# Linear attention with a soft MoE: late guards for the first three units, phases of the first batch carried on by TensorE, a new order of issue

## The chip, the cores and the metric

The kernel runs on one core of a Trainium2 chip. The time is device microseconds of one execution; three runs of the kernel before took 287.93 to 288.15 us, with a median of 288.11 us. "PE" is TensorE with its weight loads shown apart as "PEld", "DVE" is VectorE, "ACT" is ScalarE, "POOL" is GpSimd and "SP" is SyncE, whose queue issues nearly all DMAs here.

## What is computed

The reference is a gated linear attention with complex gates, followed by a soft mixture of experts. Cut to what matters:

```python
mag = sqrt(a_re**2 + a_im**2);  scale = minimum(mag, 0.999) / (mag + 1e-6)
a = scale * (a_re + 1j * a_im)                   # a gate for each token and channel
for t in range(768):                             # S is 48 x 48 for each batch and head
    S = a[t][:, None] * S + outer(k[t], v[t])
    y[t] = q[t] @ S.real
# 4 batches, 8 heads, 48 channels; y becomes x of 3072 tokens x 384
logits = x @ phi                                 # 32 slots = 8 experts x 4
slot_input = softmax(logits, 0).T @ x
slot_out = relu(slot_input @ w1[e]) @ w2[e]      # w1 384 x 1024, w2 1024 x 384
out = softmax(logits, 1) @ slot_out
```

## The kernel before, in words

**Blocks and units.** The recurrence is turned into blocks of 128 tokens. There are 24 blocks `g` (6 for each batch, `NBLK`), and three blocks make a unit `u` (`UB = 3`, 8 units). In a block the gates are used in polar form: the logarithm of the magnitude and the phase are summed over the tokens by a triangular matrix on TensorE, and q and k are multiplied by the exponentials and by the cosine and sine of the sums. Then scores, masked scores times v, and a state that is handed from block to block are ordinary matmuls.

**Gates of a unit (`gates`, L635 to L670).** The real and imaginary parts `ar` and `ai` lie in the tile `aat` (two buffers). The steps are a guard; `Ln` of `ar` in place (ACT, L647); `Exp` of its negative into the tile `gt` (ACT, L649); `ai` times that (DVE, L651); its square with a running maximum (DVE, L653); `Ln` of one plus the square (ACT, L655); their sum (DVE, L657); `Exp` (ACT, L659); and the cap (DVE, L661). `gt` has a single buffer. The guard (L642 on DVE for the first two groups, L645 on ACT for the others) reads `ar` before the logarithm overwrites it and leaves a minimum, or a sum that is zero when all is well. The first unit is gated in two groups, block 0 alone and blocks 1 and 2 together; every other unit is one group, so there are nine (`g0` to `g8`). At the end `flags` reduces the guards to one number; a branch to a slow version of the kernel hangs on it.

**Phases (`arctan`, `phase`).** After an arctangent (ACT, L677) a block's phases are summed by `up = tri_u x ph` (PE, L688), rounded (`n`, L692 or L694), and the fraction `f` is taken (DVE, L697). Sine and cosine are two ACT instructions and one DVE instruction (L702, L705, L707). A block that isn't the first of its batch needs the last block's fraction: DVE adds the last row of `f` of block g-1 to the first row of `ph` (L685, one partition), and then comes the matmul.

**Exponentials, products, attention.** `expo` is the matmul `lp` (L719, later L722) and two `Exp` (L726, L728); its last row goes by a small DMA to `rows` and comes back as `rt` (`decay`, L731, L735). `mults` makes the 128x1536 tile `hat` (DVE, L742, L747). `xpose` transposes it on PE (L759) and evicts it into `hT` (ACT, L765, DVE for block 0, L763). `score` is L770 with the masked eviction `scT` (DVE, L774), `attend` is L795 and L797 with the eviction L800, `delta` the update of the state (L808, L813, L815), `xform` a transpose of the result (L820).

**Mixture.** `logits`, `slots` and `shares` run once for a unit, then `hidden` (`H`, L241), `experts` (`X`, L271) and `combine` (`A`, L300), and twelve stores (`S`, L976).

**What sets the order.** The string `ORDER` is the order of issue, written out. Each name is one step of a generator: `p1` is the next step of `phase` for block 1, `g2` of the gates' group 2, `e`, `m`, `x`, `c`, `a`, `D` are the functions above, `T` and `L` load ScalarE's table for trigonometry or for logarithm and exponential, `la`, `lq`, `lv` load a unit's gates, q and k, and v, `w` loads 1 MB of expert weights, `d` is `decay`, and `wu` is a matmul on zeros without use ("warm-up"). `_InOrder` pins every instruction behind the one before it on its engine. So each engine and each queue runs strictly in this order and waits for the others by semaphores. PSUM tiles come from two rings: `tr` with four buffers, and `lu` with two, which `up`, `lp`, the logits and the small transposes share. Weights go through the pool `wx` with eight buffers, then through buffers that `aat`, `qkt` and other pools leave free.

Of the kernel before, what the change touches and what calls it, by code (L numbers as in the profile page):

```python
# [11 lines left out]
F32 = mybir.dt.float32  # L12
# [3 lines left out]
ALU = mybir.AluOpType  # L16
# [24 lines left out]
SPLIT, GUARD_V, ROUND_V, COPY_V = 4, 2, 4, 1  # L41
# [54 lines left out]
class _Moe:  # L96
# [216 lines left out]
    wu6 wu4 wu1 L0 wu12 wu18 i0 g0 g0 g0 g0 g0 wu17 i3 g0 g0 wu5 g0 i4 g1 g1 g1 rp1 i1 g0 e0 e0 e0 wu3 wu9 T0 t0 g1 g1 t1 e0 i2  # L313
    m0 p0 p0 p0 p0 p0 p0 L1 p1 g1 p1 m0 g1 i7 g1 wu16 i6 wu2 p1 p1 g1 p2 rp0 D0 x2 x2 p2 p2 x3 x3 p2 la0 g2 g2 g2 g2 g2 e1 e1 e1
    wu0 x1 x1 e2 e2 e2 x0 g2 T1 p1 wu14 lv0 wu10 p2 t2 D0 x0 c0 g2 c0 la1 p1 p1 p2 p2 wu15 m1 a0 p3 wu7 L2 m1 c1 c1 p3 p3 g2 g2
    x4 x4 a0 a0 x5 x5 wu13 m2 p3 e1 e2 g3 e3 e3 wu8 g3 c2 e3 g3 e5 e5 d0 m2 x10 x10 x9 e5 i8 p4 p4 x11 x11 c2 x6 x9 D0 D1 p4 x6
    g3 g3 x7 g3 x7 D1 p4 D1 p5 e4 lq0 g3 x8 x8 wu11 m3 p5 e4 e4 p5 p5 D2 c3 g3 D2 c5 c3 T2 e3 rp1 t3 p3 p3 p3 a1 a1 p6 D1 la2 p5
    p5 g3 e6 c5 p4 p5 p4 c4 m3 x12 lq1 x13 e4 D2 c4 a1 p6 m4 D3 D3 a2 p6 a2 m5 p7 p4 m4 x12 x13 D2 c6 x14 g4 c6 L3 a2 D3 l0 l0
    l0 g4 w0 e5 e6 g4 g4 e6 x14 x16 x16 x19 x19 D4 e8 x18 e8 e8 x15 x15 p7 x18 p7 g4 g4 x17 a3 x17 m5 s0 p7 p8 e7 f0 f0 g4 q0 q0
    e6 e7 e7 d1 D3 g4 f2 f2 c7 c7 c8 c8 p8 la3 q0 q0 s0 T3 p8 x20 lv1 m6 t4 lq2 p8 p7 a3 p7 p7 a3 x21 D4 p6 p6 c9 p8 x23 p9 e7  # L320
    s0 c9 p9 p6 x20 q0 a4 a4 x21 tr0 g4 m6 q0 x23 x22 x22 q0 rp0 p8 p9 c10 w1 c10 p8 D4 x27 x27 a4 g5 L4 x26 x26 s0 x25 x25 e8
    g5 c11 x24 x24 p9 D5 D5 g5 e9 m8 e9 e9 c11 e10 e10 d2 D4 a5 a5 m7 f1 f1 e10 lv2 m7 x31 x31 x28 x28 c13 m8 p10 p10 g5 g5 p10
    a5 c12 x30 p10 x29 c12 g5 e11 x29 l1 a6 x30 c13 p11 l1 a6 g5 e11 e11 m11 c14 lq3 D5 q1 q1 x34 a6 g5 c14 x34 p11 p11 m9 q1 q1
    c15 c15 T4 t5 f3 x33 p9 p10 la4 f3 D6 D6 x35 x35 p11 s0 p9 p9 D6 D6 p12 l1 p11 p11 x32 p10 s0 m9 x32 f4 f4 g5 p11 p10 a7 a7
    p12 D7 D7 q1 x33 L5 p12 m10 e9 e10 e11 c16 c16 c17 s1 a7 p13 g5 x36 x36 D7 D7 x37 x37 x38 D8 g6 c17 x38 a8 a8 g6 m10 g5 c18
    c18 q1 g6 q1 g6 g6 x42 x42 x43 x41 x41 x39 x39 e12 x43 e12 e12 D8 D8 p13 p13 p13 f5 f5 m11 x40 g6 g6 c19 c19 e14 lv3 e14 e14
    p14 d3 c21 e13 x40 D8 m12 D9 c20 e13 e13 e12 x44 s1 e13 s1 a8 a9 a9 g6 T5 c20 x44 c21 a9 p14 p14 t6 x46 x46 g6 p12 p12 D9 D9
    D9 g6 x45 x45 p14 p12 p14 p15 f7 p13 p13 p13 l2 m13 f7 l2 a10 a10 a10 m12 w2 f6 f6 c22 c22 p15 q2 p15 x47 x47 p14 p14 la5 g7
    p15 g6 x50 x50 p15 p15 p15 e14 D10 D10 lq4 d4 x51 p16 D10 c23 c23 L6 w3 x48 x51 q2 x49 m13 e15 e15 e15 x48 e15 g7 m14 m14
    a11 a11 c25 c25 p16 D11 p16 p16 D11 g7 g7 x49 p17 e16 e16 e16 x55 x57 x55 a11 e17 g7 e17 c24 e17 D11 c24 x57 l2 x54 x54 x56  # L330
    D11 p17 p17 l3 p17 g7 g7 q2 q2 l3 x52 x52 s1 x53 a12 a12 x53 x56 s1 lv4 c27 c27 la6 s1 s2 c26 c26 m15 g7 x58 x59 f8 c28 a12
    e16 a13 a13 T6 p17 p17 t7 x59 p18 p16 D12 g7 p17 p16 x58 c29 p18 a13 w4 m15 q2 D12 p16 f8 m17 x61 w5 p18 s2 c29 g8 c28 p19
# [8 lines left out]
    f17 f17 x84 x84 c41 D17 x85 c41 x86 x85 a20 x86 L9 a20 a20 m22 x88 x87 s4 m23 D18 x89 x88 D17 D18 c42 x89 x87 c43 e23 d7 D18
    q5 q5 l6 c42 w10 c43 l6 m23 a21 a21 a21 q6 D19 x92 q5 x92 q5 q6 q6 q6 x90 x90 x94 x91 q5 x91 x93 x94 D19 D18 D19 q6 c44 c44
    x95 s5 s5 c45 l6 c45 q6 D19 s5 q6 x93 c46 a22 a22 c46 x95 c47 c47 a22 a23 a23 a23 s6 s5 s5 s5 l7 l7 l7 f19 f19 q7 q7 s6 s6
    f20 f20 q7 f23 f23 q7 s7 me0 me0 s6 s6 f22 i5 s6 f21 s7 s7 f22 s7 er1 me0 f21 s7 me0 me0 me0 me0 er0 s7 ze0 q7 q7 w13 w12
# [200 lines left out]
def _polar(ctx, tc, cst, phi_sb, rp, bad, aa, qk, vv, phi, w1, w2, consts, out):  # L545
# [30 lines left out]
    amiss = cp.tile([P, len(GROUPS) - GUARD_V], F32, name="amiss")  # L576
    amin = cp.tile([P, GUARD_V], F32, name="amin")
# [57 lines left out]
    def gates(x):  # L635
# [5 lines left out]
        if x < GUARD_V:  # L641
            DVE.tensor_scalar(out=t, in0=ar, scalar1=AR_MIN, scalar2=None, op0=ALU.max, op1=ALU.min, accum_out=amin[:, x : x + 1])  # L642
        else:
            y = x - GUARD_V
            ACT.activation(out=t, in_=ar, func=AF.Relu, scale=-1.0, bias=kb[:, 3:4], accum_out=amiss[:, y : y + 1])  # L645
        yield "g1"
# [24 lines left out]

    cs, fr = {}, {}
# [6 lines left out]
    def phase(u, j):  # L679
        g = UB * u + j  # L680
        par = g % 2
        ph = aat[u][:, j, 1]
        r = slice(FIRST[par], FIRST[par] + 1)
        if g % NBLK:
            DVE.scalar_tensor_tensor(out=ph[r], in0=fr[g - 1][r], scalar=-2.0 * math.pi, in1=ph[r], op0=ALU.mult, op1=ALU.add)  # L685
            yield "p1"
        up = ps2.tile([P, HD], F32, name="up", tag="lu")
        PE.matmul(out=up, lhsT=tri_u[par], rhs=ph, start=True, stop=True)  # L688
        yield "p2"
        n = eo.tile([P, HD], F32, name="n")  # L690
        if g < ROUND_V:
            DVE.tensor_scalar(out=n, in0=up, scalar1=MAGIC, scalar2=None, op0=ALU.add)  # L692
# [9 lines left out]
        ACT.activation(out=t[:, :, 1, :], in_=f.rearrange("p (h d) -> p h d", d=D), func=AF.Sin, scale=-TWO_PI)  # L702
# [139 lines left out]
    for g in range(NG):  # L842
# [135 lines left out]
    def flags():  # L978

        good = tl.tile([P, 5], F32, name="good")  # L980
        t1 = tl.tile([P, 6], F32, name="good1")
        DVE.tensor_reduce(out=t1[:, 0:1], in_=tmax, axis=AX.X, op=ALU.max)
        DVE.tensor_reduce(out=t1[:, 1:2], in_=amiss, axis=AX.X, op=ALU.max)
        DVE.tensor_reduce(out=t1[:, 5:6], in_=amin, axis=AX.X, op=ALU.min)
# [126 lines left out]
```

## Time and profile before

| what | value |
|---|---|
| median of three runs | 288.11 us (287.93 to 288.15) |
| profiled execution | 288.15 us, of which the span is 286.3 us |
| PE busy, share of the span | 270.5 us, 94% |
| PEld busy | 216.3 us, 76% |
| DVE busy | 231.7 us, 81% |
| ACT busy | 219.3 us, 77% |
| granted clock, mean | 0.983 |
| DMA | 54.84 MB, mean 192 GB/s |
| matmul records on zeros (L923) | 38, 22.5 us busy |

The busy shares are means over stages: a start of some 40 us in which one unit's chain of steps runs with gaps, a long middle, and an end with the experts and the stores. The chain of waits tells which work ended last; the busy time of each engine in stretches tells which engine is full where. A matmul in float32 appears as two records, a transpose as one. Matmuls overlap in the records, so what one costs in a dense stream is the distance between starts, as the chain shows it, and not the duration of one record.

### The profile page before, as it was taken

How to read it: one execution, taken by the hardware profiler on the slowest of the kernel's cores; microseconds unless marked ns; L12 is line 12 of the kernel's file. 1: busy time of each engine (PE TensorE's matmuls, PEld its weight loads, DVE VectorE, ACT ScalarE, POOL GpSimd, SP SyncE). 2: the span in 40 equal slices, each digit the busy share in tenths (PEclk: the TensorE clock that was granted, in tenths of full speed). 3: DMA queues.
4: the chain of work that ended last, by engine and by line, in shares of the span. 5: the costliest groups of instructions: out<-in, count | busy, mean ns of one | idle time of the engine just before them, and what ended most of it. 6: DMA issues, size and time to landing. Idle time of an engine off the chain costs nothing.

```text
span 286.3 us, 6873 instructions
## 1 busy us (share of the span) xinstructions
PE 270.5 (94%) x2825; PEld 216.3 (76%) x2825; DVE 231.7 (81%) x422; ACT 219.3 (77%) x396; POOL 4.8 (2%) x11
## 2 busy tenths in 40 slices
PE   8869899999999999999999999999999999999970
PEld 3335568888888979989778899998979997439840
DVE  3688999999999999998899999999687765504650
ACT  3857999999999999999999998996977435110350
POOL 0200000000000000000000000000000002100000
PEclk9979999999999999999999999999999999999995
DMA  7931461910775331178749416087209497297394
GB/s 251 389 106 31 137 178 21 404 57 1 299 262 207 126 86 49 39 165 319 167 163 353 176 9 223 3 301 294 99 6 379 184 419 309 55 414 304 140 359 177
DMA packets 20198, 54.84 MB, mean 192 GB/s; under 512 B 11648, under 2 KB 12352, under 8 KB 15296
## 3 DMA queue, kind: packets, MB, share of 16 engines
q1 hardware_dynamic: 19768, 54.33, 53.3%
q8 instruction: 24, 0.39, 0.7%
q14 instruction: 14, 0.11, 0.2%
q10 hardware_dynamic: 392, 0.00, 0.1%
HBM read 49.57 MB, written 4.76 MB: 190 GB/s over the span
## 4 chain that ended last, share of the span: by engine, by line
PE 82%; DVE 5%; ACT 4%; issue 1%; DVEq 0%
PE sp L770 15%; PE tp L759 14%; PE yb L795 8%; PE db L808 8%; PE yb L797 6%; PE up L688 5%; PE xp L820 4%; PE op L271 4%; PE hp L241 4%; PE lg L118 3%; PE lp L719 2%; PE sip L185 2%; PE lp L722 2%; PE o L300 1%; PE ep L290 1%
## 5 line engine op out<-in xcount | busy, mean ns | idle before, releaser
L759 PE MATMUL tp<-cst,hat 128*96 128x128 f32 x384 | 53.2, 274 | 0.6 <-DVE hat L747 0.6
L765 ACT COPY hT<-tp 96x512 f32<-96x512 f32 x92 | 51.0, 585 | 2.8 <-PE tp L759 2.5
L770 PE MATMUL sp<-hT,hT 96*128 96x128 f32 x384 | 51.1, 279 | 0.7 <-DVE hT L763 0.7
L770 PEld LDWEIGHTS sp<-hT,hT 96*128 96x128 f32 x384 | 46.8, 192 | 5.1 <-issue 2.7
L759 PEld LDWEIGHTS tp<-cst,hat 128*96 128x96 f32 x384 | 42.3, 127 | 7.8 <-issue 4.0
L747 DVE TENSOR_TENSOR hat<-qkt,cs 128x1536 f32<-128x1536 f32 x24 | 41.9, 1751 | 0.5
L795 PE MATMUL yb<-scT,vt 128*48 128x128 f32 x384 | 36.4, 277 | 0.2 <-DVE scT L774 0.2
L774 DVE TENSOR_TENSOR scT<-sp,cst 128x512 f32<-128x512 f32 x48 | 32.3, 682 | 5.3 <-PE sp L770 5.1
L808 PEld LDWEIGHTS db<-vt,hat 128*96 128x96 f32 x320 | 31.2, 165 | 2.8 <-issue 1.6
L808 PE MATMUL db<-vt,hat 128*96 128x48 f32 x320 | 31.5, 244 | 0.0
L797 PE MATMUL yb<-hT,st 96*48 96x128 f32 x320 | 31.1, 272 | 0.0
L795 PEld LDWEIGHTS yb<-scT,vt 128*48 128x48 f32 x384 | 20.8, 122 | 6.1 <-issue 2.3
L688 PE MATMUL up<-aat,cst 128*128 128x384 f32 x48 | 20.7, 513 | 3.7 <-DVE aat L685 2.6
L923 PE MATMUL wp<-xs 128*128 128x512 f32 x38 | 22.5, 723 | 1.0 <-POOL xs L918 1.0
L742 DVE TENSOR_TENSOR qkt<-ee,qkt 128x768 f32<-128x768 f32 x24 | 22.8, 949 | 0.0
L800 ACT COPY yT<-yb 128x512 f32<-128x512 f32 x24 | 14.0, 585 | 10.3 <-PE yb L797 10.1
L797 PEld LDWEIGHTS yb<-hT,st 96*48 96x48 f32 x320 | 19.1, 123 | 0.0
L923 PEld LDWEIGHTS wp<-xs 128*128 128x128 f32 x38 | 8.4, 235 | 9.1 <-issue 6.3
L697 DVE SCALAR_TENSOR_TENSOR f<-n,up 128x384 f32<-128x384 f32 x24 | 13.2, 548 | 1.9 <-ACT n L694 1.5
L707 ACT ACTIVATE cs<-n,kb 128x384 f32<-128x384 f32 x24 | 14.3, 610 | 0.0
L820 PE MATMUL xp<-cst,yT 128*128 128x128 f32 x96 | 14.2, 276 | 0.0
L726 ACT ACTIVATE ee<-lp 128x384 f32<-128x384 f32 x24 | 11.8, 494 | 2.6 <-PE lp L722 2.4
(147 smaller groups left out, 441.7 us busy)
## 6 DMA issues: line engine op xcount, KB each, us to landing
wx<-in_w_dram SPq DMA_DIRECT2D x13, 1024.0 KB
aat<-in_aa_dram SPq DMA_DIRECT2D x7, 1152.0 KB
qkt<-in_qk_dram SPq DMA_DIRECT2D x7, 1152.0 KB
we<-in_w_dram SPq DMA_DIRECT2D x5, 1024.0 KB
vt<-in_vv_dram SPq DMA_DIRECT2D x8, 576.0 KB
aat<-in_w_dram SPq DMA_DIRECT2D x2, 1024.0 KB
qkt<-in_w_dram SPq DMA_DIRECT2D x2, 1024.0 KB
wt<-in_w_dram SPq DMA_DIRECT2D x2, 1024.0 KB
```

Of the source, the lines that this page charges most:

```text
L688: PE.matmul(out=up, lhsT=tri_u[par], rhs=ph, start=True, stop=True)
L742: DVE.tensor_tensor(out=qk, in0=ee[g], in1=qk, op=ALU.mult)
L747: DVE.tensor_tensor(out=x, in0=qk.rearrange("p w (h d) -> p w h d", d=D).unsqueeze(3).broadcast_to(sh), in1=cs[g].unsqueeze(1).broadcast_t ...
L759: PE.transpose(out=tp[:, a, :], in_=hat[g][w][:, 4 * hh + a].rearrange("p c d -> p (c d)"), identity=ident)
L765: ACT.copy(out=hT[g, hh, w], in_=tp)
L770: PE.matmul(out=sp[:, a, :], lhsT=hT[g, hh, 1][:, a, :], rhs=hT[g, hh, 0][:, a, :], start=True, stop=True)
L774: DVE.tensor_tensor(out=t, in0=sp, in1=mask[g % 2].unsqueeze(1).broadcast_to([P, 4, P]), op=ALU.mult)
L795: PE.matmul(out=o, lhsT=vt[u][:, j, h, :], rhs=scT[g, hh][:, a, :], start=True, stop=first)
L797: PE.matmul(out=o, lhsT=st[g - 1][:, h, :], rhs=hT[g, hh, 0][:, a, :], start=False, stop=True)
L808: PE.matmul(out=db[:, h, :], lhsT=hat[g][1][:, h].rearrange("p c d -> p (c d)"), rhs=vt[u][:, j, h, :], start=True, stop=True)
L820: PE.transpose(out=xp[:, c].rearrange("p a d -> p (a d)"), in_=yT[g][:, c, :], identity=ident)
L923: PE.matmul(out=wp.rearrange("p (a c) -> p a c", a=4), lhsT=blank, rhs=blank.unsqueeze(1).broadcast_to([P, 4, P]), start=True, stop=True)
```

## The change

Four things change together.

- `gates` makes no guard for units 0 to 2 (groups 0 to 3). Instead `again(u)` loads the unit's real parts a second time into a buffer of the weight pool `wx` (steps `gl0` to `gl2`, a DMA of 128 x 3 x 384 floats on SP), and a second step, much later in the order, runs the guard on ACT in place. The guard on DVE and its minimum are gone from `gates` and from `flags`.
- For blocks 1 to 5 (`CARRY = 6`) the row is no longer added by DVE. A second matmul adds it in PSUM: one partition of the 0/1 mask as weights, and the row of the last `f`. The first matmul can be issued before that `f` exists.
- The sign of `f` is turned round: the rounding multiplies by -1, and the sines and the later additions by DVE take the opposite scale.
- `ORDER` is new from end to end.

```diff
-SPLIT, GUARD_V, ROUND_V, COPY_V = 4, 2, 4, 1
+SPLIT, ROUND_V, COPY_V, CARRY, LATER = 4, 4, 1, 6, 3
...
-    amiss = cp.tile([P, len(GROUPS) - GUARD_V], F32, name="amiss")
-    amin = cp.tile([P, GUARD_V], F32, name="amin")
+    amiss = cp.tile([P, NU], F32, name="amiss")
...
-        if x < GUARD_V:
-            DVE.tensor_scalar(out=t, in0=ar, scalar1=AR_MIN, scalar2=None, op0=ALU.max, op1=ALU.min, accum_out=amin[:, x : x + 1])
-        else:
-            y = x - GUARD_V
-            ACT.activation(out=t, in_=ar, func=AF.Relu, scale=-1.0, bias=kb[:, 3:4], accum_out=amiss[:, y : y + 1])
-        yield "g1"
+        if u >= LATER:
+            guard(u, t, ar)
+            yield "g1"
...
+    def guard(u, out, ar):
+        ACT.activation(out=out, in_=ar, func=AF.Relu, scale=-1.0, bias=kb[:, 3:4], accum_out=amiss[:, u : u + 1])
+
+    def again(u):
+
+        t = wx.tile([P, W2C], F32, name="wx")[:, 0 : UB * HD].rearrange("p (j d) -> p j d", d=HD)
+        SP.dma_start(out=t, in_=aa[u][:, :, 0])
+        yield "gl1"
+        guard(u, t, t)
...
-        if g % NBLK:
-            DVE.scalar_tensor_tensor(out=ph[r], in0=fr[g - 1][r], scalar=-2.0 * math.pi, in1=ph[r], op0=ALU.mult, op1=ALU.add)
+        if g % NBLK and g >= CARRY:
+            DVE.scalar_tensor_tensor(out=ph[r], in0=fr[g - 1][r], scalar=2.0 * math.pi, in1=ph[r], op0=ALU.mult, op1=ALU.add)
             yield "p1"
         up = ps2.tile([P, HD], F32, name="up", tag="lu")
-        PE.matmul(out=up, lhsT=tri_u[par], rhs=ph, start=True, stop=True)
+        by_pe = g % NBLK and g < CARRY
+        PE.matmul(out=up, lhsT=tri_u[par], rhs=ph, start=True, stop=not by_pe)
+        if by_pe:
+            yield "p1"
+            PE.matmul(out=up, lhsT=mask[par][r, :], rhs=fr[g - 1][r, :], start=False, stop=True)
         yield "p2"
...
+    for u in range(LATER):
+        at("gl", again, u)
```

The start of the order before:

```text
wu6 wu4 wu1 L0 wu12 wu18 i0 g0 g0 g0 g0 g0 wu17 i3 g0 g0 wu5 g0 i4 g1 g1 g1 rp1 i1 g0 e0 e0 e0 wu3 wu9 T0 t0 g1 g1 t1 e0 i2
m0 p0 p0 p0 p0 p0 p0 L1 p1 g1 p1 m0 g1 i7 g1 wu16 i6 wu2 p1 p1 g1 p2 rp0 D0 x2 x2 p2 p2 x3 x3 p2 la0 g2 g2 g2 g2 g2 e1 e1 e1
wu0 x1 x1 e2 e2 e2 x0 g2 T1 p1 wu14 lv0 wu10 p2 t2 D0 x0 c0 g2 c0 la1 p1 p1 p2 p2 wu15 m1 a0 p3 wu7 L2 m1 c1 c1 p3 p3 g2 g2
x4 x4 a0 a0 x5 x5 wu13 m2 p3 e1 e2 g3 e3 e3 wu8 g3 c2 e3 g3 e5 e5 d0 m2 ...
```

and after:

```text
i0 wu17 L0 wu5 wu1 g0 g0 g0 g0 g0 g0 g0 i3 g0 i4 g1 g1 i1 tr0 i2 g1 wu7 g1 wu6 la0 e0 e0 e0 wu18 wu9 wu14 T0 t0 e0 m0 p0 p0
t1 wu13 p0 p0 p0 p0 L1 p1 p1 p1 wu8 m0 rp1 rp1 g1 g1 g1 p2 wu15 wu16 i6 p1 x3 g1 x3 wu10 p2 p2 p2 x2 g2 x2 g2 g2 i7 e1 wu3
e1 wu4 e2 e2 e2 wu12 gl0 x0 e1 x1 c1 D0 g2 g2 D0 m1 T1 lq0 rp0 t2 x0 x1 c0 p1 p1 wu11 c1 p1 p2 gl1 p2 p2 g2 gl2 p3 p3 L2 g2
la1 c0 a0 a0 a0 m1 m2 x5 x5 p3 x7 g2 x7 wu2 x4 x4 wu0 p3 m2 e1 e2 d0 D0 i8 g3 g3 g3 g3 e3 e3 e3 m3 e3 e5 e5 ...
```

Later in the new order the second steps of `gl0`, `gl1` and `gl2` stand beside blocks 13, 15 and 18. The weight loads come in the sequence `w2 e14.. d4 lq4 .. d5 w3 .. w4 w5 d6 lv6 lq6 e21 e22 w6 w7 w8 d7 w9 w10 w13 w12 w11`, where before it was `w2 .. w3 .. w4 w5 .. w6 .. w7 lq6 w8 lv6 w9 e21 e22 e23 d7 w10 w13 w12 w11`. Among the stores `S0 S2 S3 S1 S5 S4` take the place of `S3 S2 S0 S1 S4 S5`.

More of the change, by code (lines that the diff above doesn't have):

```diff
@@ L312 @@
 ORDER = """
[L313 to L332, printed above, removed]
@@ L341 @@
[L341 to L344, printed above, removed]
```

64 lines of the change are left out of this document (43 added, 21 removed).

## The prediction

> **What bounds the kernel now.** I read the page first, then the busy time by stretches, then the chain of waits.
>
> ```profile
> span 286.3 us, 6873 instructions
> ...
> PE 270.5 (94%) x2825; PEld 216.3 (76%) x2825; DVE 231.7 (81%) x422; ACT 219.3 (77%) x396; POOL 4.8 (2%) x11
> ```
>
> ```profile
> 40.00:100.00 60.00, 60.00 (x598) 51.56 (x598) 58.31 (x92) 59.49 (x102) 0.00 (x0) 1.00 0.49 175
> 100.00:150.00 50.00, 49.58 (x535) 43.29 (x535) 47.50 (x73) 49.03 (x90) 0.00 (x0) 1.00 0.48 140
> 150.00:200.00 50.00, 50.00 (x546) 44.71 (x546) 48.32 (x85) 45.28 (x85) 0.00 (x0) 1.00 0.57 194
> ```
>
> Columns of the second: stretch, length, then PE, PEld, DVE, ACT, POOL. From 40 us on three engines are full together: in 40 to 100 us PE shows 60.0, ACT 59.5 and DVE 58.3 of 60. Taking work off one gains only what the next has to spare. For PE I count by the distance of starts in the chain:
>
> ```profile
> 13.66 0.93 PE up L688 x2
> 14.61 0.57 DVE n L692
> ...
> 16.84 1.28 ACT L580
> 18.13 0.94 ACT gt L655
> ...
> 21.11 0.92 DVE aat L661
> 22.05 1.36 ACT gt L645 x2
> ...
> 24.63 1.17 ACT gt L649
> 25.83 1.37 DVE aat L651
> ...
> 28.62 1.26 ACT gt L655
> ...
> 33.88 1.77 DVE hat L747
> ...
> 39.98 0.89 PE sp L770 x8
> 40.87 0.65 PE lp L719 x2
> 41.52 0.87 PE tp L759 x8
> ...
> 43.91 0.64 PE db L808 x8
> ...
> 46.78 0.86 PE wp L923 x2
> ...
> 52.06 0.22 PE yb L795 x4
> ```
>
> Columns: start, length, step. Up to 36 us the chain hops between ACT and DVE, one gate or phase step after another; from there to 245 us it is nearly all PE. Densely, a score half costs PE 0.89 us, `lp` or `up` 0.65, two transposed halves 0.87, half a `delta` 0.64, four `yb` 0.22, a warm-up 0.86. Summing the order with these, I get 205.0 us of PE work from `lp` of block 3 (it starts at 38.25) to the first matmul of the experts (246.89):
>
> ```profile
> 38.25 0.87 PE L719 MATMUL lp<-aat,cst 128*128 128x384 f32 x2
> ```
>
> ```profile
> 246.89 10.51 PE hp L241 x96
> ```
>
> That is 208.6 us of clock, so only 3.6 us of slack in the middle. An earlier start passes through; unloading ACT and DVE there gains at most the 3.6.
>
> **The change, part by part.**
>
> *Guard of group 0.*
>
> ```profile
> 4.00 0.55 DVE L642 TENSOR_SCALAR_CACHE_REDUCE gt<-aat 128x384 f32<-128x384 f32 x1 [2.42 <-DMA aat<-in_aa_dram]
> 4.59 0.52 ACT L647 ACTIVATE aat<-aat 128x384 f32<-128x384 f32 x1 [2.57 <-DVE gt L642]
> ...
> 8.04 0.94 DVE L642 TENSOR_SCALAR_CACHE_REDUCE gt<-aat 128x768 f32<-128x768 f32 x1
> ```
>
> The load lands at 4.00, the guard holds the logarithm back to 4.59: 0.6 us. The second guard (8.04) sat between L657 and L661 of group 0 and cost about another 0.1. All steps to `up` of block 0 (13.66) are a chain, so it comes 0.7 us earlier, at 12.96. `i0`, `i3`, `i4` stay first on SP; `i1` (mask, triangle) moves up past `rp1`, and unit 1's gates move past `rp1`, `i6` and `i7`, which have over 8 us to spare.
>
> *Carry by PE.*
>
> ```profile
> 16.18 0.55 DVE L685 SCALAR_TENSOR_TENSOR aat<-f,aat 1x384 f32<-1x384 f32 x1
> ...
> 19.98 0.55 DVE L692 TENSOR_SCALAR n<-up 128x384 f32<-128x384 f32 x1
> ```
>
> ```profile
> L205 PE MATMUL mb<-cst,mrow 1*96 1x1 f32 x1 | 0.2, 202 | 0.0
> ```
>
> Five L685 of 0.55 us leave DVE (2.75 us). PE gets five more matmuls of two records. No one-partition matmul over 384 columns is in the trace; the bounds are L205 (one partition, one column, 0.2) and a full `up` (0.65). I take 0.65, the row with the same columns, type and output. By it PE gets 3.25 us, by 0.2 only 1.0. The Trainium skill, "TensorE: Matmul & The Clock Gate", section "Why this matters for your kernels", speaks against this part: it says that a single matmul over 32 rows takes as long as one over 128; no run here shows it yet. Blocks 1 to 3 are carried before the dense stretch, where warm-ups and gaps cover them; if that cover is gone they cost 1.95. Blocks 4 and 5 fall inside it: +1.3 us on the path.
>
> *The start in the new order.*
>
> ```profile
> L763 DVE COPY hT<-tp 96x512 f32<-96x512 f32 x4 | 2.6, 678 | 0.0
> ```
>
> ```profile
> 38.19 1.26 ACT L645 ACTIVATE gt<-aat,kb 128x1152 f32<-128x1152 f32 x1
> 39.35 0.19 ACT L645 ACTIVATION_READ_ACCUMULATOR gt<-aat,kb 128x1 f32 x1
> ...
> 39.82 1.15 ACT L647 ACTIVATE aat<-aat 128x1152 f32<-128x1152 f32 x1
> ```
>
> The first row is a group (count, busy, mean ns), the others are of the timeline. With the durations above (a semaphore costs 0.03 us): `up` 0 at 12.96, `n` 13.93, `f` 14.5 to 15.07. The second matmul of `up` 1 waits for `f`, and `n` 1 runs at 16.25, ahead of `hat` 0 (16.8 to 18.6). ACT loads its table at 16.15, L655 ends at 18.4; L657, `f` 1 and L661 of group 1 follow on DVE, the last to 21.5 instead of 22.0. Now the guard at 22.05: it had to wait for L661, since it wrote the single `gt`. The logarithm works in place and doesn't wait: L647 20.5 to 21.7, L649 to 22.9 instead of 25.8. But DVE first has two copies (0.67 each), `n` and `f` of block 2 (0.55 each), so L651 runs at 24.1, not 25.83: 1.7 us earlier. That lead holds to L655 (26.9 for 28.62). `hat` 1 then stands ahead of L661 of group 2, and so `lp` of block 3 leads by less: 37.55 for 38.25, 0.7 us. ACT keeps more: group 3 has no guard, and its L647 starts at 37.3 where before its guard (1.26 and 0.19) did not begin until 38.19.
>
> ACT is 2.5 us ahead there. What is late next is PE, not ACT.
>
> *New waits.* L649 of group 2 now waits for L661, with the exponentials of block 1 behind it on ACT: 0.0 to 0.2 us, because L647 ends at 21.7 and L661 at 21.5. An `up` issued early holds one of the two `lu` buffers until its `f` is taken, so `lp` of block 2 waits for `f` 2 (23.4), and behind it on PE two transposes and a score; DVE takes their results up only after 27 us. On SP `w5` waits for the first late guard, and behind it stand `d6` and the last unit's loads.
>
> *PE from there on.* After `lp` 3 the new order has two warm-ups less (-1.7), the carries of 4 and 5 (+1.3), one transposed half already done (-0.4) and one `er` pair more ahead of the experts (+0.6): 204.7 for 205.0, -0.3.
>
> *Slack.* Of the 3.6 us some comes back because ACT runs ahead and DVE has 4 us less to do (guards and L685). Bounds: 0 and 3.6. I take 0.7, near the lower end, because PE stands at 60.0 of 60 already.
>
> *The second loads and the late guards.* Three DMAs of 0.59 MB, 1.5 us each at the 385 GB/s seen below. On SP they stand behind the loads that the first blocks need, and ahead of `rp0`, `la1` and the rows of block 1; `la1` waits for `lp` of block 2 to free its buffer (about 24 us), by when they are long through, so they cost nothing; without that cover 3 x 1.5 = 4.5 us would fall on `rt`, which is not read before `D0` ends near 40 us. On POOL only `tri_t` and the two casts change places. The three guards (3 x 1.45 = 4.35 us, one of them new to ACT) fall between about 150 and 205 us, where ACT has 4.7 idle in 50. Cover: that idle time; if it is gone, a guard holds up the evictions queued behind it (`hT`, L765, then `score` on PE), up to 1.4 us each. Bounds 0 and 4.35; I take 0, the end nearest to the row with 4.7 us of room.
>
> *End.* `flags` has two DVE steps of 0.14 less, off the path. Stores S3 and S1 stand some 2.7 us of PE work later, but S9, the last, 0.6 earlier; DMA is full from 270 to 275 us (0.97, the last column but one):
>
> ```profile
> 270.00:275.00 5.00, 5.00 (x132) 4.14 (x124) 2.05 (x7) 1.75 (x5) 0.00 (x0) 1.00 0.97 385
> ```
>
> The last column is GB/s. Bounds -0.6 and +1.0; I take 0.
>
> **Sum.** -0.7 (`lp` 3) -0.3 (PE work) -0.7 (slack) = -1.7 us. The profiled execution took 288.15 us with a span of 286.3; it stands 0.04 above the median of 288.11. So 286.4 us.
>
> **The rivals.**
>
> *ACT sets the pace in the middle.* Then its whole lead counts, 2.5 us at group 3, and DVE's relief takes away the 1.0 that ACT is idle in 100 to 150 us: -3.5, 284.6 us. For it: ACT is at 59.5 of 60. Against: my count of PE's work. The Trainium skill, "Perfetto Trace Analysis", section "Identifying the Most-Contended Engine", speaks for this rival: matmul busy time is no measure, weight-load time is; that is 51.56 of 60 here, which would leave PE room.
>
> *The start isn't shorter.* Before the first `lp` stand five warm-ups instead of seven. TensorE starts at about half its rate: its weight loads fall from 0.34 to 0.19 us between 6.3 and 7.0 us. If it stays slow past 8.9 us, `lp` and `up` of block 0 take twice 0.65 each, and 1.3 of the 1.7 is lost: 287.7 us. Against: the rate rises before 8.9, and the new order fills PE from 1.0 to 8.3.
>
> ```profile
> 6.27 0.34 PEld L923 LDWEIGHTS wp<-xs 128*128 128x128 f32 x1 [0.52 <-issue]
> 7.05 0.19 PEld L923 LDWEIGHTS wp<-xs 128*128 128x128 f32 x1 [0.44 <-issue]
> ```
>
> *The late guards cost.* If half of 4.35 lands on PE: 286.4 + 2.2 = 288.6 us.
>
> *Slower: the weights come too late.* The reloads hold three of eight `wx` buffers, so `w5` to `w7` can load only after the late guards, and `w6`, `w7`, `w8` stand behind the rows of block 22.
>
> ```profile
> 212.74 0.80 SPq L735 DMA_DIRECT2D rt<-rows  x2
> ```
>
> ```profile
> 205.00:210.00 5.00, 4.97 (x52) 4.18 (x52) 4.78 (x12) 4.48 (x10) 0.00 (x0) 1.00 0.13 4
> 245.00:250.00 5.00, 4.57 (x42) 2.05 (x45) 3.27 (x18) 0.76 (x2) 0.00 (x0) 1.00 0.11 13
> ```
>
> ```profile
> 269.06 2.31 PE op L271 x78
> ```
>
> These use the idle DMA time before 215 us if they issue by about 210. If they slip behind `d7` (213 us), 3 MB more, 8 us, join the stream that feeds the experts; 4.4 us fit into 245 to 250, the rest, 3.8, delays `X`: 290.2 us. It decides at a last `wx` landing after 269 us, where `op` of the third part starts.
>
> **How the numbers follow.** Chances: forecast 0.50, ACT's pace 0.15, start not shorter 0.12, late guards 0.12, weights late 0.11. A change under 0.2% (0.58 us) can't be told from none here, so same is 287.5 to 288.7. The forecast's own range is 285.3 to 287.6. Faster takes 0.49 of the forecast, ACT's pace and a little of the start's case: 0.66. Same gets most of the start's and half of the guards' case: 0.17. Slower gets the weights and the rest: 0.17. Leaving out the weights' case and the far ends, the range is 284.3 to 289.0.
>
> **What would show it.** L647 of group 0 at 4.0; `up` 0 near 13.0; L647 of group 2 ahead of L661's end near 21.5; L651 near 24.1; `lp` 3 near 37.5; the first `hp` near 245.2. A pair of records of 0.65 for the carry. The forecast is wrong if `lp` 3 leads by under 0.3 or over 1.5 us, if PE has gaps beside the three guards, or if `hp` or `op` wait for DMA.

## The result and the profile after

The changed kernel took 285.79 us (median of six runs, 285.38 to 286.55); the kernel before, run beside it, 288.13 us (287.77 to 288.83). The ratio is 0.9917, with a 95% interval of 0.9899 to 0.9936: 2.3 us or 0.8% faster. The profiled execution took 285.81 us. (Each program mostly repeats itself closely; of the four runs of one experiment below, the guard of group 3, two took 6 us more at a lower mean clock, and only the other two are compared.)

The first two lines of the page of the changed kernel, then three stretches of the middle (columns as in the prediction; the last three are granted clock, DMA share and GB/s):

```profile
span 283.8 us, 6886 instructions
...
PE 272.3 (96%) x2835; PEld 216.4 (76%) x2835; DVE 227.9 (80%) x411; ACT 220.9 (78%) x398; POOL 4.9 (2%) x11
```

```profile
40.00:100.00 60.00, 60.00 (x601) 51.64 (x601) 57.35 (x90) 59.11 (x102) 0.00 (x0) 1.00 0.55 164
100.00:150.00 50.00, 50.00 (x542) 43.52 (x541) 48.16 (x77) 49.56 (x91) 0.00 (x0) 1.00 0.45 112
150.00:200.00 50.00, 50.00 (x547) 44.58 (x545) 47.58 (x84) 47.04 (x89) 0.00 (x0) 1.00 0.55 167
```

The middle looks as before: PE is full. DVE has 3.8 us less to do, PE 1.8 us more. The gain must be looked for where the two timelines part. Rows of the timeline of the changed kernel (start, length, engine, line; the numbers of `gates` lie 3 lower than before, so that L644 is its first logarithm, L646 its exponential, L648 the product that gives the tangent, L652 the second logarithm, L658 the cap; L731 is `lp`, L759 `hat`):

```profile
12.64 0.91 PE L696 MATMUL up<-aat,cst 128*128 128x384 f32 x2 [0.22 <-ACT aat L684]
...
19.92 1.15 ACT L644 ACTIVATE aat<-aat 128x1152 f32<-128x1152 f32 x1
20.04 0.96 DVE L658 SCALAR_TENSOR_TENSOR aat<-aat,gt 128x768 f32<-128x768 f32 x1 [0.54 <-ACT gt L656]
...
23.17 1.34 DVE L648 TENSOR_TENSOR aat<-aat,gt 128x1152 f32<-128x1152 f32 x1
...
26.20 1.27 ACT L652 ACTIVATE gt<-gt,kb 128x1152 f32<-128x1152 f32 x1
...
31.43 1.75 DVE L759 TENSOR_TENSOR hat<-qkt,cs 128x1536 f32<-128x1536 f32 x1
...
34.44 1.34 DVE L658 SCALAR_TENSOR_TENSOR aat<-aat,gt 128x1152 f32<-128x1152 f32 x1
...
35.51 1.02 PE L937 MATMUL wp<-xs 128*128 128x512 f32 x2
...
36.37 0.81 PE L731 MATMUL lp<-aat,cst 128*128 128x384 f32 x2
```

and two rows of the timeline before:

```profile
33.88 1.76 DVE L747 TENSOR_TENSOR hat<-qkt,cs 128x1536 f32<-128x1536 f32 x1
...
36.79 1.36 DVE L661 SCALAR_TENSOR_TENSOR aat<-aat,gt 128x1152 f32<-128x1152 f32 x1
```

Read them pairwise with the rows in the prediction: `up` of block 0 leads by 1.0 us (12.64 for 13.66), the second logarithm of group 2 by 2.4 (26.20 for 28.62), `hat` of block 1 by 2.45, the cap of group 2 by 2.35, and `lp` of block 3 by 1.9 (36.37 for 38.25). In the table below, the same points stand for every kernel of this study, from one profiled execution each; "Ln" is the start of the logarithm of group 2, "hat 7" the seventh `hat` to start, and the time is the median of the runs (for guard 3, whose clock is halved from 42 us on, the row is of the profiled run alone, time included).

| kernel | `up` 0 | Ln | `lp` 3 | hat 7 | first `hp` | span | time |
|---|---|---|---|---|---|---|---|
| before | 13.66 | 23.43 | 38.25 | 77.82 | 246.89 | 286.3 | 288.13 |
| changed | 12.64 | 19.92 | 36.37 | 75.29 | 244.20 | 283.8 | 285.79 |
| guards early | 14.70 | 24.76 | 41.22 | 81.53 | 250.43 | 290.1 | 290.99 |
| carry on DVE | 12.62 | 20.78 | 41.22 | 86.06 | 254.95 | 293.9 | 294.97 |
| order alone | 14.73 | 25.40 | 41.49 | 90.11 | 259.02 | 298.5 | 300.44 |
| old order | 12.73 | 20.00 | 37.31 | 78.80 | 250.35 | 289.7 | 291.49 |
| guards 0, 1 | 13.56 | 20.83 | 37.28 | 76.21 | 245.13 | 284.7 | 286.56 |
| guard 2 | 12.62 | 22.39 | 37.68 | 76.64 | 245.56 | 285.1 | 287.09 |
| guard 3 (half clock) | 12.91 | 20.19 | 36.64 | 83.37 | 252.28 | 291.7 | 293.46 |
| no late guards | 12.66 | 19.93 | 36.38 | 75.31 | 244.22 | 285.0 | 286.58 |
| before, one pause filled | 13.56 | 23.32 | 38.91 | 78.42 | 247.87 | 287.2 | 289.20 |
| order alone, filled | 14.81 | 25.47 | 41.56 | 84.79 | 253.69 | 294.4 | 296.37 |
| start moved | 12.73 | 20.00 | 35.82 | 74.75 | 243.66 | 282.4 | 284.34 |
| before, two filled, more PE | 13.59 | 23.37 | 38.18 | 77.77 | 251.05 | 291.4 | 293.37 |

Two things are read from it at once. The changed kernel has its whole lead at hat 7 (2.53 us) and loses or gains almost nothing behind it: 168.91 us to the first `hp` for 169.07, then 39.56 us to the end for 39.46. And every kernel with the new order takes 168.89 to 168.92 us from hat 7 to `hp`, whether it arrives there at 75 or at 90 us. What the start gains or loses is handed on whole, with PE full behind it (50.00 of 50 us in the rows above).

### The profile page after: what moved, and what is told of

The parts are those of the page before. It is cut to its first block, busy times and chain, and to the rows that moved or that the text cites. A ratio compares the mean times of both kernels' runs of the same rounds, so it can differ in the third digit from the quotient of the medians.

```text
span 283.8 us, 6886 instructions
## 1 busy us (share of the span) xinstructions
PE 272.3 (96%) x2835; PEld 216.4 (76%) x2835; DVE 227.9 (80%) x411; ACT 220.9 (78%) x398; POOL 4.9 (2%) x11
## 4 chain that ended last, share of the span: by engine, by line
## 5 line engine op out<-in xcount | busy, mean ns | idle before, releaser
L759 DVE TENSOR_TENSOR hat<-qkt,cs 128x1536 f32<-128x1536 f32 x24 | 42.0, 1750 | 1.2 <-PE tp L771 0.4
L937 PE MATMUL wp<-xs 128*128 128x512 f32 x38 | 21.3, 682 | 1.0 <-POOL xs L932 1.0
L696 PE MATMUL up<-aat,cst 128*128 128x384 f32 x48 | 20.0, 498 | 0.5 <-ACT ee L740 0.2
L648 DVE TENSOR_TENSOR aat<-aat,gt 128x1152 f32<-128x1152 f32 (+2 forms) x9 | 11.0, 1222 | 4.9 <-ACT gt L646 4.9
L937 PEld LDWEIGHTS wp<-xs 128*128 128x128 f32 x38 | 7.8, 220 | 8.5 <-issue 5.3
```

The costliest lines, as they stand in the source:

```text
L759: DVE.tensor_tensor(out=x, in0=qk.rearrange("p w (h d) -> p w h d", d=D).unsqueeze(3).broadcast_to(sh), in1=cs[g].unsqueeze(1).broadcast_t ...
L937: PE.matmul(out=wp.rearrange("p (a c) -> p a c", a=4), lhsT=blank, rhs=blank.unsqueeze(1).broadcast_to([P, 4, P]), start=True, stop=True)
```

## Experiments

**One part undone at a time.** Four kernels: guards back in `gates` with the new order; the carry back on DVE with the new order; both back, so that only the order is new; and the new parts in the old order, with the second loads behind the load of v of unit 1 and the late guards at `w5`, `w6`, `w7`.

```diff
 # guards early: no second loads, the guards of groups 0 and 1 on DVE, all others on ACT
-        if u >= LATER:
-            guard(u, t, ar)
+        if x < GUARD_V:
+            DVE.tensor_scalar(out=t, in0=ar, ..., accum_out=amin[:, x : x + 1])
+        else:
+            guard(x - GUARD_V, t, ar)
 # carry on DVE
-CARRY = 6
+CARRY = 0
```

> The new kernel with its guards put back into the gates (DVE for groups 0 and 1, ACT for groups 2 and 3, in the step of the logarithm), no second loads, no late guards; order and carry stay new. Theory (the guards lengthen the chain of the start): group 0 gains 0.6 us of delay, the guard of group 2 again waits for the single gt buffer and takes 1.45 us, of which about 0.9 is spare on DVE, and group 3 costs ACT 1.45; lp of block 3 comes 1.5 to 2.3 us later than 36.4 and the whole takes 287.3 to 288.1 us. Rival (the order does it): within 0.6 us of the new kernel, 285.2 to 286.4.

> The new kernel with the row of blocks 1 to 5 added by DVE again (0.55 us each), behind which the one matmul is issued where the carrying matmul stood; guards and order stay new. Theory (the carry helps the start and costs the dense stretch): lp of block 3 0.5 to 1.0 us later, since DVE is full from 18 us on and gets three more steps, and PE has 1.3 us less to do from there on: 285.3 to 286.0 us in all, so about no change. Rival (the carry is a real part of the gain): 286.5 to 287.3.

> Guards early and carry by DVE, as in the kernel before, under the new order: the order alone. Theory: the sum of the two before, 287.3 to 288.4 us, so the order alone is worth less than 1 us. Rival (the order does it): under 286.6.

> The order of the kernel before with the new parts: late guards (second loads behind the load of v of unit 1, guards beside blocks 13, 15 and 16), carry by PE, and an empty step where the guard stood. Theory: the start gains the 0.6 us of group 0 and the 1.4 us of group 2's guard, PE gets 1.3 us more: 286.4 to 287.3 us. Rival (the order does it): 287.8 to 289, because the old order issues the first matmul of a carried block no earlier than before and leaves DVE's copies where they were.

Measured: 290.99 us (ratio to before 1.0099, 1.0084 to 1.0114), 294.97 (1.0235, 1.0212 to 1.0259), 300.44 (1.0447, 1.0411 to 1.0483) and 291.49 (1.0119, 1.0101 to 1.0137). All eight expectations missed: each kernel is slower than the kernel before, by 3 to 12 us, where times from 285 to 289 us were expected. The new order with the old parts loses 12 us. So the change isn't a sum of three gains; in the two orders tried, order and parts hang together.

How a small step becomes a long wait is seen with the carry. Rows of DVE's timeline in the kernel with the carry on DVE (L694 is the carry), and the wait that PE has for it:

```profile
43.44 1.36 DVE L648 TENSOR_TENSOR aat<-aat,gt 128x1152 f32<-128x1152 f32 x1 [0.21 <-ACT gt L646]
44.83 1.36 DVE L650 CUSTOM_DVE_ANT_1 gt<-aat 128x1152 f32<-128x1152 f32 x1
...
46.12 0.95 DVE L757 TENSOR_TENSOR qkt<-ee,qkt 128x768 f32<-128x768 f32 x1
46.99 0.54 DVE L694 SCALAR_TENSOR_TENSOR aat<-f,aat 1x384 f32<-1x384 f32 x1
```

```profile
47.67 1.62 PE L699 MATMUL up<-aat,cst 128*128 128x384 f32 x2 [3.69 <-DVE aat L694]
```

A step of 0.54 us stands in DVE's queue behind three of 0.95 to 1.36 us, the first of which waited 0.21 us for ACT, and PE, which runs strictly in order too, stops for 3.69 us. Over the run PE waits 9.5 us for the five carries. In the changed kernel the same row is added by PE itself, and no `up` waits for another engine more than 0.25 us.

But the waits don't explain all of it. In the kernel with the order alone, the last column but two, the granted clock, shows something else. The stretches from 45 to 65 us:

```profile
45.00:50.00 5.00, 0.68 (x1) 0.50 (x2) 4.05 (x5) 2.51 (x7) 0.00 (x0) 0.84 0.47 31
50.00:55.00 5.00, 5.00 (x20) 3.93 (x19) 1.91 (x2) 3.83 (x6) 0.00 (x0) 0.50 0.25 89
55.00:60.00 5.00, 3.78 (x17) 2.83 (x16) 3.33 (x5) 2.79 (x4) 0.00 (x0) 0.50 0.02 0
60.00:65.00 5.00, 5.00 (x54) 4.64 (x52) 2.51 (x3) 2.83 (x5) 0.00 (x0) 0.80 0.75 240
```

After a pause of PE of 5.06 us the clock is at 0.50 for 1.6 + 5 + 5 + 2 = 13.6 us (an earlier stretch of 3.4 us, from 10.8, is in the same trace). Stretches of 3.4 us at 0.50 stand in the other three traces too: three with the carry on DVE (from 23.3, 47.2 and 54.0 us), one with the guards early (from 32.9) and one in the old order (from 21.7). So the undos price a part together with the clock that it costs. The kernel before has such a stretch too:

```profile
17.00:18.00 1.00, 1.00 (x3) 0.56 (x3) 1.00 (x1) 1.00 (x1) 0.00 (x0) 0.60 0.01 0
18.00:19.00 1.00, 1.00 (x3) 0.48 (x2) 0.61 (x1) 0.99 (x2) 0.00 (x0) 0.50 0.00 0
19.00:20.00 1.00, 1.00 (x2) 0.37 (x2) 0.90 (x2) 0.07 (x1) 0.00 (x0) 0.50 0.00 0
20.00:21.00 1.00, 1.00 (x4) 0.33 (x2) 0.97 (x3) 0.91 (x1) 0.00 (x0) 0.69 0.00 0
```

That is 0.8 + 1 + 1 + 0.6 = 3.4 us at half the rate, behind the pause from 14.57 to 16.78. In the changed kernel the clock stays at 1.00 there:

```profile
15.00:20.00 5.00, 5.00 (x16) 2.47 (x16) 3.70 (x5) 3.94 (x6) 0.00 (x0) 1.00 1.02 316
20.00:25.00 5.00, 5.00 (x17) 2.43 (x16) 4.89 (x7) 2.72 (x4) 0.51 (x1) 1.00 0.76 251
```

The prediction's reading of the start had passed over this column. It opened a new rival: the change gains because it keeps PE busy enough for the full clock.

**The guards one by one.** Three kernels put back only one place of guards each, a fourth leaves out the second loads and the late guards, so that units 0 to 2 have no guard (their sums are set to zero).

```diff
 # guards 0, 1: on DVE, group 1's ahead of the cap of group 0, no gl0
+        if x < 2:
+            DVE.tensor_scalar(out=t, in0=ar, ..., accum_out=amin[:, x : x + 1])
 # guard 2 (u == 1) or guard 3 (u == 2): in line on ACT, no gl1 or no gl2
-        if u >= LATER:
+        if u >= LATER or u == 1:
 # no late guards
-... gl0 ... gl1 ... gl2 ...
```

> The changed kernel with only the guards of groups 0 and 1 put back on DVE (no second load and no late guard for unit 0). Theory A, every guard is worth what the chain of steps loses to it: the guard of group 0 holds back the logarithm by 0.6 us, that of group 1 costs DVE about 0.9 us ahead of the cap of group 0, so `up` of block 0 at 13.4 to 14.2 us (12.64 in the changed kernel), the whole shift at the seventh `hat` and at the end: 286.5 to 287.4 us against 285.8. Theory B, the order of issue is fitted to the new parts, so a step that is late by a little makes another engine miss its turn: the shift grows along the start to more than twice the shift of `up` 0: 287.5 us or more. Theory C, PE is full anyway from 15 us on, the delay is absorbed: under 286.2 us.

> The changed kernel with only the guard of group 2 put back, in line on ACT (1.26 + 0.19 us), no second load for unit 1. It writes the single `gt` and so has to wait for the cap of group 1. Theory A: the logarithm of group 2 moves from 19.92 us to 22 to 23 us, the fourth `lp` by 1.5 to 2.5 us, and the shift passes to the end: 287.3 to 288.4 us. Theory B, coupling: more than 3 us. Theory C, PE sets the time here (5.00 of 5 us busy from 15 to 35 us): under 0.7 us, the lead that the prediction gave to `lp` of block 3.

> The changed kernel with only the guard of group 3 put back, in line on ACT (1.26 + 0.19 us), no second load for unit 2. Theory A, ACT is full at 35 to 50 us (4.97 of 5) and everything behind the guard on it moves: +1.45 us, 287.2 us, with the shift there by the seventh `hat`. Theory B, coupling: more than 2.2 us, 288 us or more. Theory C, what the prediction assumed (what is late next is PE, not ACT): under 0.4 us, 286.2 us or less.

> The changed kernel without the second loads and without the late guards: units 0 to 2 are not guarded at all. It takes 3 x 1.45 = 4.35 us off ACT in 125 to 205 us, and 1.77 MB of loads off the queue at 15 to 45 us. Theory A, as predicted, the late guards lie in idle time of ACT and the loads behind others: 0, 285.5 to 286.1 us. Theory B, ACT sets the pace of the middle: 2.2 to 4.35 us less, 281.4 to 283.6 us, gained between the 13th `hat` (126.23) and the first `hp` (244.20). Theory C, the loads on the queue delay the first blocks: a gain that is there by the seventh `hat` (75.29).

*Guards 0 and 1*: 286.56 us (ratio to before 0.9956, 0.9931 to 0.9981). `up` 0 moves by 0.92 us, and the shift is 0.91 to 0.93 at every later point of the table up to `hp`. Theory A: no growth and no absorption.

*Guard 2*: 287.09 us (0.9964, 0.9944 to 0.9984). ACT's rows show the price being made:

```profile
21.02 1.25 ACT L672 ACTIVATE gt<-aat,kb 128x1152 f32<-128x1152 f32 x1 [1.02 <-DVE aat L660]
22.18 0.19 ACT L672 ACTIVATION_READ_ACCUMULATOR gt<-aat,kb 128x1 f32 x1
22.39 1.16 ACT L646 ACTIVATE aat<-aat 128x1152 f32<-128x1152 f32 x1
```

The guard waits 1.02 us for the cap of group 1, because both use the single `gt`, then takes 1.37; the logarithm starts 2.47 us later. Of that 1.31 reaches `lp` 3 and 1.36 the end of the middle. That is nearest to theory A, a little under its 1.5 to 2.5 and its 287.3 us.

*Guard 3*: 287.03 and 287.14 us in the two runs compared (0.9965, 0.9935 to 0.9995). Set against the 285.79 of the changed kernel, the guard's price is 1.3 us, near the 1.45 of theory A; theory C, that ACT is not late here, fails. PE's rows show where it falls, first of the changed kernel, then with the guard:

```profile
39.36 0.91 PE L696 MATMUL up<-aat,cst 128*128 128x384 f32 x2 [0.23 <-ACT ee L740]
```

```profile
41.01 0.91 PE L698 MATMUL up<-aat,cst 128*128 128x384 f32 x2 [1.61 <-ACT ee L742]
```

`lp` 3 is still within 0.3 us of the changed kernel's, and then `up` waits 1.61 us for ACT, where it waited 0.23. Behind 42.2 us the trace is not read, since its clock is then at 0.50 up to 55.9.

*No late guards*: 286.58 us (0.9949, 0.9929 to 0.9969). ACT has 3.1 us less to do in this one stretch,

```profile
150.00:200.00 50.00, 50.00 (x547) 44.59 (x545) 47.58 (x84) 43.97 (x83) 0.00 (x0) 1.00 0.56 167
```

and the first `hp` comes at 244.22 for 244.20. Neither the loads nor the guards cost anything, and ACT doesn't set the pace of the middle. (The total is above theory A's range because of the end: from the first `op` to the last instruction it took 29.3 us for 28.1. Between kernels with the same order there it ranged from 27.3 to 29.3. A part is a pause of PE ahead of one `ep` or `op` that waits for nothing the trace shows: 0.5 us in the changed kernel, 1.0 here, 1.8 with the order alone filled, none with the start moved. What makes it, no experiment here tells.)

**The clock.** Warm-ups in PE's pauses change nothing else. Into the kernel before, two ahead of `up` 1; into the kernel with the order alone, ten at four places; then the kernel before with both its pauses filled, and in another stage 48 transposes more.

```diff
 # before, one pause filled
-... L1 p1 g1 p1 m0 ...
+... L1 p1 g1 wu19 wu20 p1 m0 ...
 # order alone, filled: 2 ahead of e0, 1 ahead of the second p1, 2 of the second p2, 5 of the second p4
 # before, two filled (also wu21 wu22 ahead of the up of block 2), and in xform:
-        for c in range(4):
+        for c in list(range(4)) * (2 if 6 <= g < 18 else 1):
```

> The kernel before with two more warm-ups ahead of the `up` of block 1, in the pause that PE makes from 14.57 to 16.78 us (2 x 0.86 = 1.72 of 2.2 us). In the kernel before the granted clock is 0.5 for 3.41 us (17.4 to 20.8) right after that pause; in the changed kernel it never is between 7 and 275 us. Theory A, the start is a chain of ACT and DVE steps and the half clock lay beside it: 287.8 to 288.2 us, no change. Theory B, the half clock cost PE up to half of 3.41 us there, so that a large part of the change's 2.3 us is the clock: 286.3 to 287.4 us, with the stretch of half clock gone. Theory C, the pause isn't what drops the clock: the stretch at 0.5 stays.

> The run with the new order alone (guards early, carry on DVE, 300.4 us) with ten more warm-ups in PE's pauses: two ahead of the first `lp`, one ahead of the `up` of block 1, two ahead of that of block 2, five ahead of that of block 4 (pauses of 2.50, 1.35, 2.32 and 5.06 us). That run had the clock at 0.5 for 3.41 and then for 13.65 us; at half the rate these cost up to 8.5 us. Theory A, most of what it lost is the clock, dropped by the pauses: no stretch of half clock, 291 to 293.5 us. Theory B, it lost the time because steps miss their turn in the order, and the clock follows from that: 298 us or more, whatever the clock. Theory C, the clock falls all the same, since the pauses come again elsewhere: about 300 us or above.

> The kernel before with two edits in separate stages, read separately by the seventh `hat` (77.82 us) and the first `hp` (246.89 us). First, two warm-ups ahead of the `up` of block 1 and two ahead of that of block 2, so that both pauses of the start are filled (the run that filled the first alone had its stretch of half clock 4.8 us later, after a pause of 2.03 us). Second, the four transposes of `xform` are made twice for blocks 6 to 17: 12 x 0.44 = 5.3 us of PE work that nothing needs, between 126 and 212 us. Start, theory A: no stretch of half clock, and the seventh `hat` at 77.5 to 78.2 us, since the half clock lay beside the path; theory B: 76.0 to 77.2 us, the half clock cost up to 1.7 us. Middle (169.07 us from the seventh `hat` to the first `hp`), theory A: PE sets the pace without slack, 174.0 to 174.5 us; theory B, the 3.6 us of slack that the prediction counted are there: 170.5 to 171.5 us; theory C, ACT or DVE sets the pace: 169 to 169.5 us. The total is 288 us plus the two differences.

*One pause filled*: 289.20 us (1.0029, 1.0017 to 1.0040), slower. The half clock went from 17.2 to 23.3 us, behind the next pause (20.39 to 22.42):

```profile
15.00:20.00 5.00, 4.51 (x19) 2.26 (x18) 4.29 (x7) 3.26 (x5) 0.00 (x0) 1.00 0.20 66
20.00:25.00 5.00, 2.97 (x12) 1.91 (x11) 4.38 (x8) 3.91 (x5) 0.00 (x0) 0.83 0.00 0
25.00:30.00 5.00, 5.00 (x17) 2.47 (x16) 4.18 (x6) 3.35 (x6) 0.00 (x0) 0.83 0.15 28
```

There `lp` 3 is 0.66 us later. None of the three theories had that: the stretch is gone from its place, but a new one stands elsewhere, so A and B stayed open, which led to the third kernel.

*Two filled*: the clock is at 1.00 throughout,

```profile
15.00:20.00 5.00, 4.50 (x19) 2.23 (x18) 4.29 (x7) 3.25 (x4) 0.00 (x0) 1.00 0.29 103
20.00:25.00 5.00, 4.68 (x18) 2.40 (x17) 4.56 (x8) 3.88 (x5) 0.00 (x0) 1.00 0.00 0
```

and hat 7 comes at 77.77 us for 77.82. Theory A: in the kernel before the half clock lay beside the chain of ACT and DVE steps and cost nothing. The gain over the kernel before is not the clock. The second edit of that kernel adds 48 transposes; the doubled groups take 0.87 to 0.97 us where the single ones took 0.44 to 0.63, by these spans some 5.0 us of PE work in all, and the middle grows by 4.2 us (173.28 for 169.07). PE's room in the middle is thus about 0.8 us, between theory A (none) and theory B (3.6); it is an estimate, since the same order with one pause filled took 169.45 us there.

*Order alone, filled*: 296.37 us (1.0302, 1.0277 to 1.0326). The clock stays full, and PE's waits shrink; the first row is of the unfilled kernel, the second of the filled:

```profile
PE up L704 <- DVE aat L699: 10.7, 5, 5.1
```

```profile
PE up L704 <- DVE aat L699: 3.2, 4, 1.4
```

(total wait, times, longest; warm-ups now stand where PE waited.) Hat 7 comes 5.3 us earlier, but is still 9.5 us behind the changed kernel. Between theories A and B: about a third of the loss was the clock (4.1 of the 14.7 us behind the changed kernel, 5.3 of 14.8 by hat 7). The rest is put down to the waits of the chain itself, guards (0.9 + 1.35 + 1.3 us by the single undos) and carries on DVE; it was not split further.

**A better start.** If a lead at the start passes whole to the end, the rows of the changed kernel show where more is to be had: from 20.9 to 34 us DVE is nearly full (it waits 0.44 us once), with two copies for block 0 between the gates' steps, while ACT waits 1.87 us for `lp` of block 2, which stands behind two warm-ups.

```diff
-... x2 g2 x2 g2 g2 i7 e1 wu3 e1 wu4 e2 e2 e2 wu12 gl0 x0 e1 ...
+... x2 g2 g2 x2 g2 i7 e1 e1 e2 wu3 e2 wu4 e2 gl0 x0 e1 ...
-        if g < COPY_V:
+        if g < COPY_V and (hh, w) != (1, 0):
             DVE.tensor_copy(out=hT[g, hh, w], in_=tp)
```

> The changed kernel with a few moves between 21 and 26 us and nothing else: the copy of the fourth `tp` of block 0 goes to ACT behind the exponential of group 2 (ACT has 0.45 and 1.87 us idle there, DVE is full), the two warm-ups ahead of `lp` of block 2 stand behind it (ACT waits 1.87 us for it), and the third warm-up there is left out. Theory A, DVE sets the time from 21 to 34 us and a lead at the start passes whole to the end: the tangent product of group 2 (L648) near 22.6 us instead of 23.17, the third `hat` 0.6 to 0.9 us earlier, and as much at the end, 284.9 to 285.3 us. Theory B, something else is late by 36 us (ACT or the PSUM ring): no gain, 285.6 to 286 us. Theory C, with a warm-up less PE pauses, and the clock falls: 287 us or more.

Measured: 284.34 us (0.9865, 0.9851 to 0.9879), against 0.9899 to 0.9936 for the changed kernel. Rows of its timeline (line numbers are one higher):

```profile
22.25 0.56 ACT L778 COPY hT<-tp 96x512 f32<-96x512 f32 x1
22.65 1.35 DVE L649 TENSOR_TENSOR aat<-aat,gt 128x1152 f32<-128x1152 f32 x1
...
25.44 1.26 ACT L653 ACTIVATE gt<-gt,kb 128x1152 f32<-128x1152 f32 x1 [0.44 <-DVE tmax L651]
...
34.96 1.02 PE L938 MATMUL wp<-xs 128*128 128x512 f32 x2
...
35.82 1.45 PE L732 MATMUL lp<-aat,cst 128*128 128x384 f32 x4
```

The product comes at 22.65 as forecast, the third `hat` 0.82 us earlier; a warm-up ahead of `lp` 3 takes back 0.27, and 0.55 us is handed on to `hp`, again to the hundredth. So the lead passes on as theory A has it, but smaller, and the total lies below its range. The rest of the 1.4 us lies in the end of the kernel (27.3 us from the first `op` for 28.1; 27.5 to 29.3 in the other kernels of this order), where nothing was edited, and is not claimed.

## Why the prediction was right, and where its sum was not

The forecast was 286.4 us, and 285.8 came. The direction and the way were right: a lead won at the start that passes through a full PE. The sizes were not: -0.7 at `lp` 3, -1.0 behind it and 0 at the end were forecast, -1.88, -0.81 and +0.10 came. By the prediction's own sign (wrong if `lp` 3 leads by over 1.5 us) its walk of the start failed; that the total stayed in its range, 0.5 us from the edge, owes something to the width of the range. By its own steps:

- *Guard of group 0*, `up` 0 at 12.96: 12.64. Undoing this part alone gives 0.92 us where the prediction had 0.7. In the kernel before, `lp` 0 also stood behind warm-ups (8.93 for 10.05), which the step did not count.
- *The start in the new order*: the mis-sized term. `lp` of block 3 was to lead by 0.7 us; it leads by 1.88. It failed twice. L648 came at 23.17, not 24.1, and the lead at the second logarithm was 2.4, not 1.7: 0.3 us of that was there at `up` 0 already, and 0.4 arose in the five DVE steps ahead of L648, where the walk added 0.03 us between instructions of one engine while their records overlap (DVE's 20.04 for 0.96, 20.92 for 0.68, 21.52). Then the prediction took away 1.0 because "`hat` 1 then stands ahead of L661 of group 2". It does so in the kernel before as well (33.88 and 36.79, the two rows above); the cap kept 2.35 of the lead, and only a warm-up in front of `lp` 3 (35.51) took 0.5.
- *ACT keeps 2.5 us, but what is late next is PE*: the logarithm of group 3 led by 3.6 (36.19 for 39.82). At this place the step failed: with the guard of group 3 back on ACT, PE waits for ACT at 41 us and 1.3 of the 1.45 us come through, so ACT was late next there. Further on, in the middle, ACT's time doesn't count, as the prediction had it (no late guards: 0.02 us).
- *PE work -0.3, slack -0.7*, from `lp` 3 to `hp`: -0.81 together (207.83 for 208.64), nearly all of it before hat 7. The room itself, counted as 3.6, is about 0.8 as far as the doubled transposes of blocks 6 to 17 tell; so the 205.0 us of PE work were counted some 2.8 us too low, or PE has waits that the count left out.
- *Carry by PE*, taken at the price of a full `up`, 0.65: near, and a little low. The group's records (count, busy, mean ns) beside those of a full `up`:

```profile
L696 PE MATMUL up<-aat,cst 128*128 128x384 f32 x48 | 20.0, 498 | 0.5 <-ACT ee L740 0.2 <-ACT aat L684 0.2
...
L700 PE MATMUL up<-f,cst 1*128 1x384 f32 x10 | 4.5, 533 | 0.0
```

  and two rows of PE's timeline:

```profile
40.20 0.91 PE L700 MATMUL up<-f,cst 1*128 1x384 f32 x2
41.04 0.91 PE L731 MATMUL lp<-aat,cst 128*128 128x384 f32 x2
```

  One row of weights costs no less than 128 rows. By the distance of starts, the prediction's measure, a carry takes 0.84 us. The Trainium skill, "TensorE: Matmul & The Clock Gate", section "Why this matters for your kernels", gives a single matmul over 32 rows the time of one over 128, and the records here agree for one row. What the prediction didn't see is what the carry buys: with the row on DVE in the new order, PE stops for up to 3.7 us.
- *Second loads and late guards, 0*: right, 0.02 us. Their place seems to matter: with the same guards at other places in the old order the middle took 171.55 us for 169.07, and the lag grew where two of the guards ran, near 161 and 191 us; this was not tried apart.
- *End, 0*: +0.10 us. The weights came as argued: two went out at 203.85, right behind the rows of block 22 and before the 210 us of the rival, and the last five behind the first `hp`, with DMA full (1.01) from 245 to 260 us and no wait of `hp` or `op` for them.

```profile
203.85 2.41 SPq L631 DMA_DIRECT2D wx<-in_w_dram  x2
...
246.16 3.76 SPq L631 DMA_DIRECT2D wx<-in_w_dram  x5
```

```profile
245.00:260.00 15.00, 15.00 (x230) 7.65 (x226) 4.37 (x13) 1.47 (x3) 0.00 (x0) 1.00 1.01 419
```

Of the rivals none came. *ACT sets the pace*: refuted for 150 to 200 us by the run without late guards. The rule of the Trainium skill, "Perfetto Trace Analysis", section "Identifying the Most-Contended Engine", that TensorE's headroom is judged by weight-load time (or the share of peak arithmetic) and not by matmul busy time, spoke for it with 51.6 of 60 us; here the trace differs, since some 5 us more of transposes cost 4.2 us. *The start isn't shorter*: the rate was full by 7 us.

## What to carry to other kernels

Where three engines run strictly in order, walk the start step by step, and where one engine is full behind it give a lead at its end its full value: here at most 0.02 us of a lead or a lag of up to 15 us was lost over the next 169 us. A part of a change that is worth little by itself can be what makes an order possible, so undoing one part doesn't give its price. Even the guards didn't add up: put back one place at a time they cost 0.8, 1.3 and 1.3 us, and all together 5.2 us, with a stretch of half clock besides. Read the clock column in the stretches where PE still has pauses: filling all of them cost nothing in the kernel before (hat 7 at 77.77 for 77.82) and won 4.1 us in the order alone, while filling one of two moved the half clock to a place where it did harm.

## What the runs showed of the hardware

- The half clock comes in stretches of 3.4 us (the kernel before, one pause filled, guards early, carry on DVE, old order) or 13.6 us, four times that (order alone, guard 3). Its falls keep to the same step: with the carry on DVE they lie at 23.3, 47.2 and 54.0 us, seven and two times 3.41 us apart, and in the kernel before the weight loads quicken at 7.0 us and the clock falls at 17.2, three steps later. So it may matter how a pause lies to these steps, whose start differs from run to run. The Trainium skill, "TensorE: Matmul & The Clock Gate", section "What's actually happening", has a free-running window of about 3.4 us, which fits the shorter stretch; it speaks of an idle window, but here the clock fell behind pauses of 2.2 us (before), 2.0 (one pause filled) and 1.6 (guard 3). In the filled kernel of the order alone a pause of 1.7 us dropped nothing, while in the old order the clock fell at 21.7 us with no pause above 1.1 us ahead of it. PE's busy time in the 3.41 us ahead doesn't settle it either: 1.20 us (before) and 2.61 (old order) with a fall, 1.68 (order alone filled, from 13.0 us) without. What decides was not tried.
- Between hat 7 and the first `hp`, ten kernels of one order agree within 0.03 us over 169 us, at the full clock.
- When PE reaches its full rate differs from run to run: with the same warm-ups at the same times (one starts at 3.71 us in each), weight loads fell from 0.34 to 0.19 us by 5.1 us with guard 3, by 5.2 with the start moved, and at 7.0 in the changed kernel. The first `lp` came at 9.20, 9.02 and 8.93, so it made no difference here.
